# Products of two SBUF tensors offered to GpSimd, and a new table of due dates, in a planned three-stage kernel

## The chip, the cores and the metric

One core of a Trainium2 chip runs the whole program. The metric is the device time of one execution in microseconds (us). Timed executions are given as a median of three; a further execution is recorded by the hardware profiler, and the rows below come from that one.

## What is computed

The reference chains three stages over 4 batches of 768 steps (3072 tokens), 8 heads of 48 columns.

```
for t in range(S):                                   # linear attention with decay w and bonus u
    cur = einsum('bhd,bhe->bhde', u * k_t, v_t)
    y_t = einsum('bhd,bhde->bhe', r_t, state + cur)
    state = w * state + einsum('bhd,bhe->bhde', k_t, v_t)
x = y.transpose(0, 2, 1, 3).reshape(B * S, H * D)
h = x @ w_in                                         # 384 -> 2048
x = softplus(h) @ w_out                              # 2048 -> 384
logits = x @ w_gate                                  # 8 experts, 384 places each
# greedy assignment by falling logit; then, for each expert e,
out[mask] = maximum(x[mask] @ w1[e], 0) @ w2[e]      # 384 -> 1024 -> 384
```

## The kernel before

**Tiling.** The attention is done in 24 steps (called n, 0 to 23), each with 64 time steps of two batches on the 128 partitions. A step loads r, k and v into the tiles rn, kn and vn (two buffers of each, so step n + 2 uses the buffers of step n). It makes ks = kn x pwn[1] and rs = rn x pwn[0], tables of powers of the decay, turns them with TensorE (kT, ar), multiplies them (the masked part goes back into ar), updates the state (wx, copied to X) and multiplies ar with X. The bonus term needs rk = rn x kn, then rk x ut (called rk*ut below), then a sum over columns (sd) that scales vn into sv. Steps 0 to 2 make the bonus on TensorE instead. The sum xf becomes xhl, a pair of float16 halves, and a DMA turns it into xt. Three steps make one block of 384 tokens. Each of the 8 blocks goes through the first feed-forward layer (ffn1, TensorE line 879, 16 slices; ScalarE lines 889 to 891 and VectorE lines 896 and 903 make the softplus) and the second (ffn2, lines 1010 to 1012). The float64 weights of these layers are taken apart on VectorE first (lines 786 to 790). Then the tokens are chosen expert by expert, gathered, multiplied (lines 1504 and 1522 to 1524) and scattered.

**What sets the order.** Nothing is issued as it is written. Every piece of work is recorded as an item with an engine, a planned duration, its dependencies and a due date. `lay_out` then plans all engines once while the program is built: the engine that can start first takes, among the items that could start within SLACK of that moment, the one with the smallest due date plus its entry in the table NUDGE. Items that name several engines in a dictionary go to the one that could start them first, with a handicap: YIELD for VectorE, and BIAS times the difference of planned durations. So each engine's order is fixed when the program is built, and on the chip each engine works through its order and waits on semaphores.

**The shared port in the plan.** The planner keeps a time for VectorE and one for GpSimd in `port`: an item that touches SBUF only on one of them is not planned beside such an item on the other. An item marked `remote` waits for the other's time but doesn't set its own, so that what follows on the other engine may be planned beside it.

```
if eng in port and eng in it.port and not it.remote:
    port[eng] = it.done
```

**Fillers.** Where the plan leaves TensorE without work, `keep_warm` puts matmuls of the tile still into bank 7 (line 184), one for each 56 ns of the planned gap.

**The products.** `product` (line 416) makes ks and rs of steps 1 to 23, and rk and rk*ut of steps 3 to 23: 46 + 42 = 88 products of 128 x 384 float32. Their helper is one line, so the profile has all of them as L416. The zero stores are four items of 96 KB that write zeros to rows of x2d which are read by the first gather.

Of the kernel before, what the change touches and what calls it, by code (L numbers as in the profile page):

```python
# [21 lines left out]
def tile_kernel(ctx, tc, r, k, v, w, u, w_in, w_out, w_gate, w1, w2, out):  # L22
# [18 lines left out]
    PE, ACT, DVE, POOL, SP = nc.tensor, nc.scalar, nc.vector, nc.gpsimd, nc.sync  # L41
# [11 lines left out]


    LAT = 150.0
    SLACK = 87.403
    SAME = {"dve": 130.0, "act": 150.0}
    NBANK = 7
    BIAS = 1.853
    YIELD0 = 218.503  # L60
    YIELD = {"dve": YIELD0}
    WARM = 1e9
    LPH = 6
# [18 lines left out]
    PAIR = (500.0, 1000.0, 2)  # L82
    LANES = 8
    NUDGE = {
# [24 lines left out]
    }  # L109
    LIMIT = {"ph": LPH, "p2": LP2, "att": LATT, "sel": LSEL, "pt": LPT}  # L110
    items, writer, readers = [], {}, {}
# [4 lines left out]
    def banks_of(bank):  # L116
        return [] if bank is None else bank if isinstance(bank, list) else [bank]
# [32 lines left out]
    def op(eng, dur, fn, r=(), w=(), due=0.0, lat=None, bank=None, size=None, small=0):  # L150
        deps = []
        if lat is None:
            lat = LATA[0] if GROUP[0] == "att" else LAT
        for key in r:
            deps.append(writer.get(key))
        for key in w:
            deps.append(writer.get(key))
            deps += readers.get(key, [])
        for b in banks_of(bank):
            deps += b.items  # L160
        it = Item(eng, dur, fn, deps, due, lat, [b for b in banks_of(bank) if not b.items], bank, size)
        for b in banks_of(bank):
            if eng == "pe":
                b.items = [it]
            b.items = b.items[:1] if eng != "pe" else b.items
            b.all.append(it)
        it.small = small
        for key in r:
            readers.setdefault(key, []).append(it)
        for key in w:  # L170
            writer[key] = it
            readers[key] = []
        return it
# [15 lines left out]
    def lay_out(todo, rank, clock, warm=False):  # L189
# [19 lines left out]
        def when(it, eng):  # L209
            at = it.at  # L210
            if eng in port and eng in it.port:
                at = max(at, port["pool" if eng == "dve" else "dve"])
            if len(it.could) > 1:
                at += YIELD.get(eng, 0.0) + BIAS * (it.could[eng] - min(it.could.values()))
            if it.size and eng != "pool":
                k = len(landed) + it.size[2] - 1 - LANES
                if k >= 0:
                    at = max(at, landed[k])
            for b in it.banks:
                for e, t in b.last.items():  # L220
                    if e != eng and eng != "pe":
                        at = max(at, t + LAT)
            if not it.take:
                return at
            k = len(it.take) - 1
            return max(at, sorted(bank_at)[k], sorted(class_at[it.take[0].cls])[k])
# [7 lines left out]
        while any(ready.values()):  # L234
            start, eng = INF, None
            for e, ls in ready.items():
                if ls:
                    t = max(clock[e], min(when(it, e) for it in ls))
                    if t < start:
                        start, eng = t, e  # L240
            it = min((i for i in ready[eng] if when(i, eng) <= start + SLACK),
                     key=lambda i: ((i.small != small) + (not i.small) if eng == "pe" and small else 0, *rank(i)))
# [72 lines left out]
    def begins(blk):  # L315
        return T0 if blk <= 0 else T0 + LEN0 + (blk - 1) * LEN
# [17 lines left out]
    PARTED = 8  # L334
    QUEUES = 1
    UDUE = 2000.0
    ZERODUE = 30000.0
    UTDUE = 6000.0
    HALFL = 12965.117
    HALFL2 = 16904.146  # L340
# [72 lines left out]
    x2d = dram.tile([N, 2 * DM], HF, name="x2d")  # L413

    def product(o, a, b, r, w, due):
        op("dve", 470.0, lambda: DVE.tensor_mul(o, a, b), r=r, w=w, due=due)  # L416


    def scaled(eng, o, a, by):
# [16 lines left out]
    def load_step(n):  # L436
# [52 lines left out]
       w=["gate"], due=T0, size=SMALL)  # L489
# [28 lines left out]
    def factors():  # L518
# [8 lines left out]
       r=["pwt", ("ar", 1, 0)], w=["pwh", ("kT", 1)], due=-1e8)  # L527
    op("dve", 350.0, lambda: DVE.tensor_tensor(PW2[0][..., :C // 2], pwt[:, :, None, :].to_broadcast(twice),
                                               rec[:, :, None, None].to_broadcast(twice), op=OP.mult),
       r=["pwt", ("ar", 1, 0)], w=["pw"], due=-1e8)  # L530
# [22 lines left out]
    def attention(n):  # L553
# [8 lines left out]
        if n:  # L562
            product(ks[:, :, :D], KN[i], PWN[1][:, :, :D], knk + [("pwn", 1), "pads"], [("ks", i)], due)
            product(rs[:, :, :D], RN[i], PWN[0][:, :, :D], rnk + [("pwn", 0), "pads"], [("rs", i)], due + 1)
# [114 lines left out]
        def bonus():  # L679
            product(rk, RN[i], KN[i], rnk + knk, ["rk"], due + 3)  # L680
            product(rk, rk, ut.rearrange("p (h d) -> p h d", h=H), ["ut"], ["rk"], due + 3)
            op("dve", 470.0, lambda: DVE.tensor_reduce(sd, rk, axis=AX.X, op=OP.add), r=["rk"], w=[("sd", i)], due=due + 3)
            op({"dve": 470.0, "act": 1700.0}, 0.0, weighted, r=vnk + [("sd", i)], w=[("sv", i)], due=due + 3)
# [304 lines left out]
    for i in range(2 * NG):  # L988
        b0, s0 = step_tok(NS - NG + i // 2)
        X2S.append(op("sp", 650.0, lambda row=(b0 + i % 2) * S + s0: SP.dma_start(x2d[row:row + 64, :], none),  # L990
                      r=["none"], due=begins(0) + ZERODUE, size=STORE))

# [638 lines left out]
```

## Time and profile before

| | us |
|---|---|
| median of 3 executions (lowest, highest) | 718.51 (718.35, 718.58) |
| the profiled execution | 720.05 |
| its span, first to last instruction | 718.2 |
| around the span | 1.85 |
| mean granted TensorE clock in the span | 0.997 of full speed |

The span is what the rows below divide. The profiled execution took 1.54 us more than the median of the timed ones.

### The profile page before, as it was taken

Reading aid. Unit: us, or ns where it says so; the run is one execution under the profiler, and the core shown is the slowest. Engines: PE = TensorE matmul, PEld = TensorE weight load, DVE = VectorE, ACT = ScalarE, POOL = GpSimd, SP = SyncE. Lnnn points to the kernel's source line nnn. Section 1 sums busy time; section 2 is a strip of 40 time slices with the busy share of each in tenths; the row PEclk is TensorE's granted clock in tenths of the full one; section 3 lists DMA queues with packets and bytes.
Section 4 is the critical chain, followed back from the end, with each engine's and each line's share of the span. In section 5 each row is a group of like instructions: output and inputs, shape, how many; then the busy total and the mean of one; then the engine's idle time right before and its main releaser. Section 6 shows DMA issues by size and latency. Waiting matters only on the chain.

```text
span 718.2 us, 18288 instructions
## 1 busy us (share of the span) xinstructions
PE 707.8 (99%) x7173; PEld 458.5 (64%) x7173; DVE 604.0 (84%) x1638; ACT 401.7 (56%) x889; POOL 63.4 (9%) x107
## 2 busy tenths in 40 slices
PE   9999999999899999999999999999999999999996
PEld 8986666657666666666666566666666665566663
DVE  6999999999898968988899868887799898988630
ACT  4588698674398712689999801311345533524530
POOL 3000000000000000000010000001212422313211
PEclk9999999999999999999999999999999999999998
DMA  6985972445741426512010003442358667647900
GB/s 120 267 202 155 237 149 38 90 86 116 124 77 23 74 52 127 75 29 43 15 23 1 1 13 111 122 143 57 102 143 212 192 155 201 195 124 210 265 34 33
DMA packets 165015, 79.65 MB, mean 111 GB/s; under 512 B 132801, under 2 KB 158273, under 8 KB 164929
## 3 DMA queue, kind: packets, MB, share of 16 engines
q1 hardware_dynamic: 159216, 68.56, 42.0%
q0 software_dynamic: 3072, 9.44, 3.7%
q8 instruction: 56, 0.92, 0.5%
q10 hardware_dynamic: 2640, 0.49, 0.4%
q14 instruction: 31, 0.25, 0.1%
HBM read 60.37 MB, written 9.83 MB: 98 GB/s over the span
## 4 chain that ended last, share of the span: by engine, by line
PE 64%; DVE 15%; issue 12%; DMA 3%; POOL 3%; ACT 2%; POOLq 0%; SPq 0%; DVEq 0%
PE bank L879 20%; PE bank L1010 6%; PE bank L1012 6%; PE bank L1011 6%; PE bank L1504 6%; PE bank L1007 3%; DVE ar L625 2%; PE bank L720 2%; PE bank L184 2%; PE bank L1522 2%; PE bank L1524 2%; PE bank L1523 2%; POOL out L1532 2%; PE bank L615 1%; PE bank L588 1%
## 5 line engine op out<-in xcount | busy, mean ns | idle before, releaser
L879 PEld LDWEIGHTS <-wi 128*128 128x128 f16 x1008 | 98.0, 98 | 65.3 <-issue 1.1
L879 PE MATMUL bank<-xt,wi 128*128 128x384 f16 x672 | 127.6, 326 | 0.1
L1010 PE MATMUL bank<-wo,g 128*128 128x384 f16 (+1 forms) x240 | 78.5, 327 | 0.0
L1012 PE MATMUL bank<-wo,g 128*128 128x384 f16 (+1 forms) x240 | 78.5, 327 | 0.0
L1011 PE MATMUL bank<-wo,g 128*128 128x384 f16 (+1 forms) x240 | 78.4, 327 | 0.0
L879 PE MATMUL bank<-xs,wi 128*128 128x384 f16 x336 | 72.9, 326 | 0.0
L1504 PE MATMUL bank<-g,w1h 128*128 128x384 f16 x384 | 72.8, 325 | 0.0
L889 ACT ACTIVATE ta<-bank 128x384 f32<-128x384 f32 x128 | 61.5, 481 | 17.2 <-PE bank L879 12.9
L896 DVE SCALAR_TENSOR_TENSOR gf<-bank,ta 128x384 f32<-128x384 f32 x112 | 61.6, 551 | 11.2 <-ACT ta L891 10.0
L891 ACT ACTIVATE ta<-ta 128x384 f32<-128x384 f32 x128 | 66.6, 522 | 1.7
L890 ACT ACTIVATE ta<-ta 128x384 f32<-128x384 f32 x128 | 66.4, 522 | 1.5
L1524 PE MATMUL bank<-w2h,g 128*128 128x384 f16 x192 | 62.6, 326 | 0.0
L1523 PE MATMUL bank<-w2l,g 128*128 128x384 f16 x192 | 62.5, 326 | 0.0
L1522 PE MATMUL bank<-w2h,g 128*128 128x384 f16 x192 | 62.5, 326 | 0.0
L1508 ACT ACTIVATE g<-bank 128x384 f16<-128x384 f32 x64 | 31.2, 489 | 43.1 <-PE bank L1504 29.2
L421 ACT ACTIVATE x2o<-bank 128x384 f16<-128x384 f32 x23 | 11.3, 493 | 72.8 <-PE bank L1012 65.3
L1504 PEld LDWEIGHTS <-w1h 128*128 128x128 f16 x384 | 35.5, 97 | 22.9 <-issue 1.0
L903 DVE SCALAR_TENSOR_TENSOR g<-gf,g 128x384 f16<-128x384 f32 x80 | 43.2, 549 | 2.9 <-ACT g L421 2.2
L1511 DVE SCALAR_TENSOR_TENSOR g<-bank,g 128x384 f16<-128x384 f32 x64 | 34.4, 547 | 11.0 <-ACT g L1508 11.0
L1504 PE MATMUL bank<-g,w1l 128*128 128x384 f16 x192 | 41.7, 326 | 0.0
L625 DVE TENSOR_TENSOR ar<-bank,mask 64x256 f32<-64x256 f32 x84 | 35.4, 421 | 4.5 <-PE bank L615 2.7
L1429 POOL DMA_INDIRECT third<-x2d,idx x24 | 25.1, 1044 | 150.7 <-PE bank L1317 124.8
(251 smaller groups left out, 1403.9 us busy)
## 6 DMA issues: line engine op xcount, KB each, us to landing
mraw<-moe_w SPq DMA_DIRECT2D x64, 384.0 KB
third<-moe_w_out SPq DMA_DIRECT2D x8, 768.0 KB
third<-moe_w_in SPq DMA_DIRECT2D x6, 768.0 KB
x2d<-x2o SPq DMA_DIRECT2D x48, 96.0 KB
vn<-v SPq DMA_DIRECT2D x47, 96.0 KB
rn<-r SPq DMA_DIRECT2D x46, 96.0 KB
kn<-k SPq DMA_DIRECT2D x46, 96.0 KB
X<-v SPq DMA_DIRECT2D x36, 96.0 KB
```

Of the source, the lines that this page charges most:

```text
L879: PE.matmul(ph, WF[:, f, a, kk, :], x[:, kk, :], start=(i == 0), stop=(i == 3 * KC - 1))
L889: op("act", 371.0, lambda: ACT.activation(ta, bank.view(BT), AF.Abs), w=[("ta", c)], due=due, bank=bank)
L890: op("act", 413.0, lambda: ACT.activation(ta, ta, AF.Exp, scale=-1.0), w=[("ta", c)], due=due)
L891: op("act", 413.0, lambda: ACT.activation(ta, ta, AF.Ln, bias=1.0), w=[("ta", c)], due=due)
L896: op("dve", 470.0, lambda: DVE.scalar_tensor_tensor(gf, bank.view(BT), 0.0, ta, op0=OP.max, op1=OP.add), r=[("ta", c)], w=[("gf", c)], due ...
L1010: PE.matmul(p, gh[:, f, ts], WU[:, f, 0, :no], start=(f == 0), stop=False)
L1011: PE.matmul(p, gh[:, f, ts], WU[:, f, 1, :no], start=False, stop=False)
L1012: PE.matmul(p, gl[:, f, ts], WU[:, f, 0, :no], start=False, stop=(f == FC - 1))
L1504: PE.matmul(ph, a[:, kk, fs], XH[p][:, x0 + kk, :], start=(i == 0), stop=(i == 3 * KC - 1))
L1522: PE.matmul(po, h1h[:, f, js], w2h[:, fz, :], start=(f == 0), stop=False)
L1523: PE.matmul(po, h1h[:, f, js], w2l[:, fz, :], start=False, stop=False)
L1524: PE.matmul(po, h1l[:, f, js], w2h[:, fz, :], start=False, stop=(f == FB - 1))
```

## The change

A product may now go to GpSimd or VectorE: it names both, at a planned 1150 ns and 490 ns (before 470 ns on VectorE alone), and is marked remote. The due date of the zero stores is moved by 90 us. Three numbers of the planner change a little, and the whole table NUDGE is replaced. Lines behind line 416 of the kernel before stand three lines further down in the changed kernel.

```diff
-    SLACK = 87.403
+    SLACK = 89.403
...
-    BIAS = 1.853
-    YIELD0 = 218.503
+    BIAS = 1.9579999999999997
+    YIELD0 = 207.503
...
     NUDGE = {
-        0: -143448, 1: -197030, 4: -22082, 15: -11678, 16: -12043, 17: -29443, 18: -24752, 19: -1000149502, 20: -1000062522, 21: -10145293,
...
+        1: -363201, 16: -21377, 17: -95815, 18: -86229, 19: -1000139052, 20: -99951731, 21: -10237327, 23: -999934724, 24: -999961413, 43:
...
-    ZERODUE = 30000.0
+    ZERODUE = 120000.0
...
     def product(o, a, b, r, w, due):
-        op("dve", 470.0, lambda: DVE.tensor_mul(o, a, b), r=r, w=w, due=due)
+        op({"dve": 490.0, "pool": 1150.0}, 0.0, lambda eng: (POOL if eng == "pool" else DVE).tensor_mul(o, a, b), r=r, w=w, due=due).remote = True
```

**GpSimd's order, from the factors uw to the first table of the selection.** Before, no product stands here; X_97 is the state that is cleared for step 12.

```order
L519 MEMSET uw 128x8
L521 TENSOR_TENSOR uw<-uq,wt 48x4 x2
L568 MEMSET X_97 64x384
L569 MEMSET X_97 64x384
L1090 IOTA io 128x384
```

In the changed kernel the first products stand behind uw: rs and ks of step 3, rk*ut of step 3, ks and rs of step 5, rk*ut of step 4, ks of step 6, rs and rk of step 9 and rs of step 12.

```order
L522 MEMSET uw 128x8
L524 TENSOR_TENSOR uw<-uq,wt 48x4 x2
L419 TENSOR_TENSOR rs_101<-rn_92,pwn_146 128x8x48
L419 TENSOR_TENSOR ks_103<-kn_94,pwn_147 128x8x48
L419 TENSOR_TENSOR rk_104<-rk_104,ut 128x384
L419 TENSOR_TENSOR ks_103<-kn_94,pwn_147 128x8x48
L419 TENSOR_TENSOR rs_101<-rn_92,pwn_146 128x8x48
L419 TENSOR_TENSOR rk_104<-rk_104,ut 128x384
L419 TENSOR_TENSOR ks_102<-kn_93,pwn_147 128x8x48
L419 TENSOR_TENSOR rs_101<-rn_92,pwn_146 128x8x48
L419 TENSOR_TENSOR rk_104<-rn_92,kn_94 128x384
L419 TENSOR_TENSOR rs_100<-rn_91,pwn_146 128x8x48
```

28 of the 88 products have moved to GpSimd: 11 stand ahead of the clearing of X_97 and 17 behind it; 60 stay on VectorE.

**VectorE's order around ks of step 14.** Before, that product (ks_102) has these rows ahead of it, from rs of step 15 on; wx_113 is the state of step 13 here, and rk_104 the bonus of step 14 (the state of step 12 stands just ahead of these rows).

```order
L416 TENSOR_TENSOR rs_101<-rn_92,pwn_146 128x8x48
L1027 TENSOR_SCALAR LG<-bank_85 128x8
L423 TENSOR_SCALAR xs_120<-xt_118 128x3x128
L423 TENSOR_SCALAR x2o_131<-bank_85 128x384
L416 TENSOR_TENSOR rk_104<-rn_91,kn_93 128x384
L1023 SCALAR_TENSOR_TENSOR x2o_131<-bank_85,x2o_131 128x384
L625 TENSOR_TENSOR ar_112<-bank_86,mask 64x4x64 x2
L653 TENSOR_TENSOR wx_113<-bank_80,wx_113 128x4x48
L416 TENSOR_TENSOR rk_104<-rk_104,ut 128x384
L657 TENSOR_TENSOR wx_113<-wx_113,w_144 128x384
L682 TENSOR_REDUCE sd_105<-rk_104 128x8
L416 TENSOR_TENSOR ks_102<-kn_93,pwn_147 128x8x48
```

In the changed kernel ks of step 14 stands right behind the state of step 12 (bank_82 into wx_113).

```order
L685 TENSOR_REDUCE sd_105<-rk_104 128x8
L419 TENSOR_TENSOR rs_101<-rn_92,pwn_146 128x8x48
L419 TENSOR_TENSOR rk_104<-rn_92,kn_94 128x384
L628 TENSOR_TENSOR ar_112<-bank_83,mask 64x4x64 x2
L654 TENSOR_TENSOR wx_113<-bank_85,w_144 128x4x48
L654 TENSOR_TENSOR wx_113<-bank_82,w_144 128x4x48
L419 TENSOR_TENSOR ks_102<-kn_93,pwn_147 128x8x48
L432 COPY X_98<-wx_113 64x384
L1026 SCALAR_TENSOR_TENSOR x2o_132<-bank_81,x2o_132 128x384
L426 TENSOR_SCALAR xs_120<-xt_118 128x3x128
L1030 TENSOR_SCALAR LG<-bank_81 128x8
L685 TENSOR_REDUCE sd_106<-rk_104 128x8
```

The whole of step 13's state and of step 14's bonus has moved from ahead of ks to behind it or earlier; rk*ut of steps 13 and 15, rs of step 14 and ks of step 15 are now GpSimd's.

## Rows read from the trace of the kernel before

**Rows 1.** The page, sections 1 and 2: engines over the span; tenths in 40 slices

```profile
PE 707.8 (99%) x7173; PEld 458.5 (64%) x7173; DVE 604.0 (84%) x1638; ACT 401.7 (56%) x889; POOL 63.4 (9%) x107
...
DVE  6999999999898968988899868887799898988630
...
DMA  6985972445741426512010003442358667647900
```

**Rows 2.** Busy time by stretch: stretch, length, PE, PEld, DVE, ACT, POOL, clock, DMA, GB/s

```profile
30.00:60.00 30.00, 29.99 (x390) 25.30 (x382) 29.33 (x59) 24.86 (x61) 0.00 (x0) 1.00 0.88 210
60.00:100.00 40.00, 40.00 (x443) 26.78 (x444) 39.27 (x78) 31.24 (x78) 0.00 (x0) 1.00 0.88 194
100.00:150.00 50.00, 49.85 (x495) 30.82 (x493) 49.69 (x115) 41.02 (x104) 0.00 (x0) 1.00 0.38 82
150.00:200.00 50.00, 48.17 (x728) 32.21 (x727) 46.69 (x112) 25.10 (x59) 0.82 (x2) 1.00 0.57 105
200.00:300.00 100.00, 100.00 (x1179) 64.00 (x1178) 85.67 (x198) 60.21 (x144) 0.00 (x0) 1.00 0.42 73
```

**Rows 3.** Waits of PE in the whole span: us in total, times, longest

```profile
PE bank L646 <- DVE ks L416: 1.0, 1, 1.0
PE bank L720 <- DVE ar L625: 0.8, 1, 0.8
```

**Rows 4.** Groups by line: the fillers on PE

```profile
L184 PE MATMUL bank<-still 128*128 128x128 bf16 x204 | 16.1, 235 | 1.0 <-DVE wt L479 1.0
```

**Rows 5.** Timeline of DVE around 187 us: start, us, work

```profile
184.20 0.56 DVE L416 TENSOR_TENSOR rk<-rn,kn 128x384 f32<-128x384 f32 x1 [0.63 <-DMA kn<-k]
...
186.04 0.62 DVE L653 TENSOR_TENSOR wx<-bank,wx 128x192 f32<-128x192 f32 x2
186.58 0.55 DVE L416 TENSOR_TENSOR rk<-rk,ut 128x384 f32<-128x384 f32 x1
...
187.98 1.02 DVE L416 TENSOR_TENSOR ks<-kn,pwn 128x384 f32<-128x384 f32 x2
...
189.49 0.88 DVE L625 TENSOR_TENSOR ar<-bank,mask 64x256 f32<-64x256 f32 x2
```

**Rows 6.** Timeline of PE around 187 us

```profile
187.30 0.33 PE L1012 MATMUL bank<-wo,g 128*128 128x392 f16 x1
188.58 0.68 PE L646 MATMUL bank<-vn,ks 64*64 64x48 f32 x32 [0.95 <-DVE ks L416]
```

**Rows 7.** Groups by line: products, scalings and the second half of g

```profile
L416 DVE TENSOR_TENSOR rs<-rn,pwn 128x384 f32<-128x384 f32 x23 | 12.6, 549 | 1.4 <-DMA rn<-r 1.4
...
L421 ACT ACTIVATE g<-gf 128x384 f16<-128x384 f32 x40 | 20.7, 519 | 2.9 <-DVE gf L896 2.8
...
L423 DVE TENSOR_SCALAR g<-gf 128x384 f16<-128x384 f32 x40 | 14.5, 362 | 0.7
...
L903 DVE SCALAR_TENSOR_TENSOR g<-gf,g 128x384 f16<-128x384 f32 x80 | 43.2, 549 | 2.9 <-ACT g L421 2.2
```

**Rows 8.** Timeline of POOL in the first 7 us

```profile
1.89 0.56 POOL L502 TENSOR_SCALAR identf<-jp 128x128 f32<-128x128 int32 x1
...
5.05 0.41 POOL L574 MEMSET X<- 64x384 f32 x1
...
5.99 0.58 POOL L574 MEMSET X<- 64x384 f32 x1
```

**Rows 9.** Timeline of DVE in the same time

```profile
5.77 0.44 DVE L429 COPY ar<-kT 128x512 f32<-128x512 f32 x1
```

**Rows 10.** Timeline of PE at a change of matmul shape

```profile
230.40 0.33 PE L1011 MATMUL bank<-wo,third 128*128 128x392 f16 x1
230.56 0.33 PE L1012 MATMUL bank<-wo,third 128*128 128x392 f16 x1
230.82 0.68 PE L646 MATMUL bank<-vn,ks 64*64 64x48 f32 x32
```

**Rows 11.** Timeline of SP's queue: the zero stores' first pair

```profile
19.65 2.13 SPq L990 DMA_DIRECT2D x2d<-third  x2
```

49 rows, old and new, of the table NUDGE are left out of this document.

## The prediction

> **What bounds the kernel now.** I read the page first. TensorE's matmuls are busy for 707.8 of 718.2 us, VectorE for 604.0, and GpSimd for 63.4 [rows 1]. But busy matmuls overlap, so 99% doesn't say that nothing is left: the fillers count as busy too. The 204 fillers are busy for 16.1 us, 0.079 us each [rows 4]; 52 of them stand ahead of the first real matmul, while the first loads arrive, which the change leaves as they are. So only the other 152 fillers, about 12 us at 0.079 us each, and the waits of TensorE can be won at all. The rest of the matmuls is the same before and after.
>
> Next I read the stretches, to see where VectorE could be what TensorE waits for. From 30 to 150 us VectorE is busy for 29.33 of 30, 39.27 of 40 and 49.69 of 50 us: it is full. From 150 to 200 us it is busy for 46.69 of 50, and TensorE for 48.17, its largest gap outside the two ends; from 200 to 300 us VectorE has 14 us to spare and TensorE none [rows 2]. Up to 100 us DMA is just as full, 0.88 of its time in both stretches [rows 2]. So relief for VectorE can move the end only if it falls before 200 us, and up to 100 us perhaps not even there.
>
> Then the waits of TensorE by name: two are left that VectorE ends, 1.0 us of L646 for ks and 0.8 us of L720 for ar [rows 3]. Both lie near 187 us: after the last ffn2 matmul at 187.30 us the state matmuls of step 14 start at 188.58 us, 0.95 us of it counted as idle [rows 6]. VectorE has no gap just then. It runs rk, the state, rk*ut and only then ks, at 187.98 us, and reaches the ar that L720 waits for at 189.49 us [rows 5]. This is a queue on VectorE, and products make up much of it.
>
> **What the change does, part by part.**
>
> *Products.* 28 of 88 go to GpSimd. One takes VectorE 549 ns [rows 7], so VectorE loses 28 x 0.549 = 15.4 us. The planner then gives VectorE other work in their place: by the order it makes 8 more scalings (L423), 7 more copies (L429) and 2 more state and bonus scalings, and ScalarE correspondingly fewer. At 0.362 us for a scaling [rows 7], about 0.4 for a copy (the one of 512 columns takes 0.44 [rows 9]) and 0.55 for the others that is 2.9 + 2.8 + 1.1 = 6.8 us. VectorE ends 8.6 us lighter, near 595 us busy. ScalarE loses 8 x 0.519 = 4.2 us for the scalings [rows 7] and some for the rest. ScalarE is not what bounds any stretch [rows 2], so I count that as nothing; the cover is its own idle time, 5 us even in the fullest of these stretches (24.86 of 30).
>
> *Price on GpSimd.* No row shows a product of this shape on GpSimd. From below: a memset of 384 columns, which reads nothing, takes 0.41 us; from above: 128 columns of one input take 0.56 us, and three times that is 1.7 us [rows 8]. I take 1.15 us, the number in the new line, which lies well between; 28 of them fill 32 us of an engine that is idle for 655 us. GpSimd's order has nothing behind the products that is urgent before the gathers, except the clearing of X for step 12 (11 products ahead of it, 17 behind).
>
> *Where it counts.* 11 products leave VectorE before about 165 us, 11 x 0.55 = 6 us, where it is full. I don't credit these: with DMA at 0.88 [rows 2] and, in the new order, 54 fillers still standing among the matmuls of the weight stretch, against 49 before, TensorE is expected to wait for the weights there as it does now. What I credit is the place at 187 us. In the new order ks of step 14 stands right behind the state of step 12. Three products and the state of step 13 that preceded it are elsewhere. I take the whole first wait, 0.95 us [rows 6], and half of the second, 0.4 of 0.8 us [rows 3], since the ar products themselves remain: -1.35 us. Bounds: nothing (a late load takes the place of the queue), and both waits, -1.8 us.
>
> *Changes of matmul shape.* TensorE pays for going from full to small tiles: matmuls of L1011 and L1012 start 0.16 us apart, but the first small one starts 0.26 us after the last of L1012 [rows 10], so 0.1 us a change. The order has 102 such changes before and 92 after: 10 x 0.1 = -1.0 us. Bounds: nothing, where such a change hides a wait that remains, and twice that, -2 us.
>
> *Fillers.* 209 against 204: 5 x 0.079 [rows 4] = +0.4 us at most, nothing if they only fill idle time.
>
> *Zero stores.* By their new due date they would start 90 us later. In SP's order they move only by a few rows: eight DMAs stand between the third and the fourth weight load before (the four stores among them) and eight after (loads of the attention and one store). The first pair takes SP 2.13 us to issue [rows 11], and as much is put in its place, so 0 us. Without that cover it would be one weight load 2 us later or earlier, in the stretch where DMA is full.
>
> *Sum.* -1.35 - 1.0 + 0.4 = -1.95 us. Against the profiled execution, 718.2 us of span and 1.85 around it, 720.05 - 1.95 = 718.1 us. The median of the timed runs stands 1.54 us below the profiled one, so the forecast is 718.5 - 1.95 = **716.6 us**. A change of 0.2%, 1.4 us, is about what a measurement of this kernel can tell from none.
>
> **A rule against it.** What one engine's SBUF access does to the other shows in one place: the memset of X at 5.99 us takes 0.58 us instead of 0.41 [rows 8], while VectorE's copy from SBUF to SBUF runs from 5.77 to 6.21 us [rows 9]. So GpSimd waited for VectorE, for about 0.17 us. The Trainium skill, "SBUF — State Buffer", section "Who interferes with whom", says that a VectorE instruction with two SBUF inputs, or in a two-port mode, and a GpSimd instruction that reads SBUF exclude each other, and that the second to start is blocked until the first has ended. By that rule the products are not free beside VectorE. The trace agrees for a copy that blocks GpSimd; no row shows VectorE held, because GpSimd makes no such product. By the trace's 0.17 us the sum stays; by the rule it is the second rival.
>
> **Rivals.**
>
> *No change that can be told.* The relief up to 200 us is eaten by loads. For it: DMA at 0.88 while VectorE is full [rows 2], and rk at 184.20 us waited 0.63 us for a load of kn [rows 5], so around 187 us loads are late as well. Against it: the fewer shape changes need no relief. Only a part of the 1.0 us and the fillers remain: 718.5 - 0.5 = 718.0 us.
>
> *Slower: VectorE is held by GpSimd's products.* The second half of g, L903, with both inputs in SBUF, runs 80 times at 549 ns [rows 7], and with it the weight preparation, the scalings from SBUF and the remaining products: about every second VectorE instruction could be held. A product of 1.15 us covers two of them, so one is met by most products, and has to wait for something between 0 and 1.15 us, 0.6 to 0.7 on average. For the 11 products in the full stretch that is 7 us more against 6 us saved, and about a third of the 6.8 us taken over from ScalarE, 2.3 us, falls there too: VectorE ends this stretch 3 us late. From 200 us on TensorE has no gap in which to recover [rows 2], so nearly all of it arrives at the end: 718.5 + 3.3 - 1.0 = 720.8 us. The 17 later products cost nothing by themselves, with 14 us of VectorE's time free in 100 [rows 2]. It decides from the point where the mean hold passes the 0.55 us that each product saves.
>
> *The change doesn't do what it says* is excluded: the order shows the 28 products on GpSimd.
>
> **How the numbers follow.** The forecast has 0.43, no change 0.31, held VectorE 0.26. The forecast's own range: both waits gone and 2 us for the shapes, 718.5 - 3.8 = 714.7 us, up to 717.1 us, the bound of what can be told. Holds of the full 1.15 us would add 11 x 0.5 = 5 us to the slower case; half of that is 723, which I leave out together with the far end of the gains. Range 714.5 to 721.6 us. Faster by over 0.2%: 0.43; within: 0.31; slower: 0.26.
>
> **What would show it.** Right: 28 rows of L419 on POOL near 1.15 us each; VectorE's products still near 549 ns, and scalings near 362 ns; VectorE busy near 595 us; no wait of L649 for ks of step 14; the stretch from 150 to 200 us without TensorE's gap of 1.8 us. Wrong: L906 or the products on VectorE with a longer mean or gaps in front of them while POOL runs L419; products on POOL of 1.7 us and more; transposes (L591) waiting for a POOL product; new fillers' stretches followed by waits for weight loads; the clearing of X for step 12 late behind products that wait for a load.

## The result, and the profile after

The changed kernel takes 723.6 us (median of 4 runs, 723.44 to 725.02), the kernel before 718.43 (4 runs) beside it: a ratio of 1.0069, 95% interval 1.0058 to 1.0081. It is slower by about 5 us, where 716.6 was forecast, and it lies outside the range of 714.5 to 721.6. The profiled execution took 723.44 us with a span of 721.6. In the changed kernel the product is L419, the scaling L426, the second half of g L906; in the experiments an edit that adds lines shifts the numbers further (gf, L899 here, is L906 in E2 and L911 in E11 and E12).

First the page of the changed kernel, section 1, which answers to [rows 1].

```profile
PE 710.1 (98%) x7178; PEld 460.7 (64%) x7178; DVE 605.0 (84%) x1627; ACT 397.3 (55%) x862; POOL 92.4 (13%) x135
```

GpSimd is 29 us busier and ScalarE 4.4 us lighter, about as expected. But VectorE, which gave away 28 products, is busy for 605.0 us, 1 us more than before. The forecast had 595. That is the first line to stop at.

The same kernel by stretch; the columns are those of [rows 2].

```profile
30.00:60.00 30.00, 28.86 (x424) 25.05 (x422) 29.22 (x56) 26.57 (x67) 3.96 (x4) 1.00 0.84 205
60.00:100.00 40.00, 39.78 (x455) 26.04 (x454) 39.54 (x76) 30.98 (x85) 0.00 (x0) 1.00 0.93 213
100.00:150.00 50.00, 49.30 (x451) 30.87 (x449) 49.43 (x111) 41.05 (x97) 2.28 (x2) 1.00 0.36 74
150.00:200.00 50.00, 49.21 (x530) 31.07 (x529) 41.85 (x95) 26.71 (x61) 6.06 (x7) 1.00 0.34 63
200.00:300.00 100.00, 98.95 (x1354) 64.73 (x1353) 85.61 (x200) 54.96 (x127) 11.40 (x11) 1.00 0.50 93
```

TensorE's gap from 150 to 200 us shrinks from 1.83 to 0.79 us, as predicted, but the stretch no longer holds the same work: the state matmuls of steps 12 to 14, at 177 to 189 us before, stand at 202 to 214 us now. New gaps stand at 30 to 60 (1.14 us), 100 to 150 (0.70) and 200 to 300 us (1.05), where there was next to nothing [rows 2].

The waits of TensorE name who ends them (us in total, times, longest):

```profile
PE bank L649 <- DVE gf L899: 0.7, 1, 0.7
PE bank L753 <- DVE xf L740: 0.6, 1, 0.6
PE bank L882 <- DVE x2o L1026: 0.5, 1, 0.5
PE bank L618 <- DVE gf L899: 0.5, 1, 0.5
PE bank L882 <- DVE wx L656: 0.5, 2, 0.3
PE bank L875 <- DVE wi L793: 0.5, 1, 0.5
```

The two waits of [rows 3] are gone. These six have come, all ended by VectorE, 3.3 us in sum.

What does VectorE do beside a product on GpSimd? The timeline of GpSimd in the changed kernel:

```profile
27.01 1.04 POOL L419 TENSOR_TENSOR rk<-rk,ut 128x384 f32<-128x384 f32 x1 [5.35 <-DMA ut<-u]
...
127.85 1.32 POOL L419 TENSOR_TENSOR rk<-rn,kn 128x384 f32<-128x384 f32 x1
...
198.79 1.00 POOL L419 TENSOR_TENSOR rs<-rn,pwn 128x384 f32<-128x384 f32 x1 [29.57 <-PE bank L591]
...
206.69 1.00 POOL L419 TENSOR_TENSOR ks<-kn,pwn 128x384 f32<-128x384 f32 x1 [2.67 <-PE bank L649]
```

and of VectorE at the same times:

```profile
26.16 0.55 DVE L791 SCALAR_TENSOR_TENSOR wi<-third,wi 128x384 int32<-128x384 int32 x1
26.63 0.55 DVE L660 TENSOR_TENSOR wx<-wx,w 128x384 f32<-128x384 f32 x1
27.10 1.37 DVE L793 SCALAR_TENSOR_TENSOR wi<-third,wi 128x384 int32<-128x384 int32 x1
...
127.60 0.71 DVE L419 TENSOR_TENSOR ks<-kn,pwn 128x384 f32<-128x384 f32 x1
128.24 1.35 DVE L677 TENSOR_TENSOR sv<-vn,sd 128x384 f32<-128x384 f32 x1
...
199.05 0.96 DVE L426 TENSOR_SCALAR xhl<-xf 128x384 f16<-128x384 f32 x1
...
206.35 0.54 DVE L685 TENSOR_REDUCE sd<-rk 128x8 f32<-128x384 f32 x1
206.91 1.31 DVE L628 TENSOR_TENSOR ar<-bank,mask 64x256 f32<-64x256 f32 x3
```

Read the two together. GpSimd starts at 27.01 us and ends at 28.05; L793 starts at 27.10 on VectorE and ends at 28.47, 0.42 us after GpSimd. Its own work of 0.55 us has been pushed back until GpSimd was done. The same holds for L677 (1.35 instead of 0.55) and for a scaling with one input, L426 (0.96 instead of 0.36 [rows 7]). All ten two-input instructions of 384 or 392 columns that were pushed back end 0.41 to 0.43 us after the product that held them. At 206.69 us nothing is pushed: a reduction was running, then three L628, which read a bank of PSUM, 1.31 us for three in a row. GpSimd suffers as well: 1.32 us at 127.85, where VectorE's ks was running first.

Over the 28 products, 13 instructions on VectorE are longer by more than 0.1 us than their kind is undisturbed, 6.9 us in sum (0.16 to 0.83 each). 15 products hold nothing; beside them stand reductions, work on banks, and instructions that were running first.

### The profile page after: what moved, and what is told of

The parts are those of the page before. It is cut to its first block, busy times and chain, and to the rows that moved or that the text cites. A ratio compares the mean times of both kernels' runs of the same rounds, so it can differ in the third digit from the quotient of the medians.

```text
span 721.6 us, 18319 instructions
## 1 busy us (share of the span) xinstructions
PE 710.1 (98%) x7178; PEld 460.7 (64%) x7178; DVE 605.0 (84%) x1627; ACT 397.3 (55%) x862; POOL 92.4 (13%) x135
## 4 chain that ended last, share of the span: by engine, by line
PE 72%; issue 11%; DVE 8%; ACT 4%; POOL 3%; SPq 1%; DMA 0%; POOLq 0%; DVEq 0%
PE bank L882 20%; PE bank L1013 7%; PE bank L1015 7%; PE bank L1014 7%; PE bank L1507 7%; PE bank L1010 4%; PE bank L723 2%; PE bank L1525 2%; PE bank L1526 2%; PE bank L1527 2%; PE bank L187 2%; POOL out L1535 2%; PE bank L591 1%; PE bank L649 1%; PE bank L618 1%
## 5 line engine op out<-in xcount | busy, mean ns | idle before, releaser
L899 DVE SCALAR_TENSOR_TENSOR gf<-bank,ta 128x384 f32<-128x384 f32 x112 | 61.5, 552 | 11.9 <-ACT ta L894 10.8
L906 DVE SCALAR_TENSOR_TENSOR g<-gf,g 128x384 f16<-128x384 f32 x80 | 43.4, 551 | 2.4 <-ACT g L424 1.7
L1466 DVE SCALAR_TENSOR_TENSOR w2l<-mraw,w2h 128x768 f16<-128x768 f32 x32 | 30.4, 953 | 9.2 <-ACT w2h L1462 9.2
```

Source lines behind the costliest of these rows:

```text
L899: op("dve", 470.0, lambda: DVE.scalar_tensor_tensor(gf, bank.view(BT), 0.0, ta, op0=OP.max, op1=OP.add), r=[("ta", c)], w=[("gf", c)], due ...
```

## The experiments

Each ratio is to runs of the kernel before on the same chip, whose medians there are 719.33 us (E1, E2, E4, E5), 719.19 (E6, E7, E8, E10) and 719.14 (E11, E12, E13).

### E1: the new order, all products on VectorE

```diff
-        op({"dve": 490.0, "pool": 1150.0}, 0.0, lambda eng: (POOL if eng == "pool" else DVE).tensor_mul(o, a, b), r=r, w=w, due=due).remote = True
+        op({"dve": 490.0, "pool": 1150.0}, 0.0, lambda eng: DVE.tensor_mul(o, a, b), r=r, w=w, due=due).remote = True
```

> The changed kernel with its order kept, but the 28 products that the plan gives to GpSimd are issued on VectorE at the same places. No GpSimd product is left, so VectorE is held nowhere, and it gets 28 x 0.55 = 15.4 us of work back. Theory A (the loss is VectorE held by GpSimd's products, 6.9 us in all in the trace of the changed kernel): the holds go, the work comes back, and where both fall in the full stretches it is a net loss of some 4 us: 724 to 728 us. Theory B (the new order itself loses the time, at 27 to 85 us and 195 to 230 us, with or without holds): also 724 to 728 us, or more. The run measures what the offer to GpSimd is worth in this order: at 723.6 us or less it is worth nothing.

Measured: 725.09 us, ratio 1.0088 (1.0072 to 1.0105). Its page:

```profile
PE 709.8 (98%) x7178; PEld 459.8 (64%) x7178; DVE 611.1 (85%) x1655; ACT 396.9 (55%) x862; POOL 62.9 (9%) x107
```

The order takes VectorE 611.1 - 604.0 = 7.1 us more when it makes everything itself; that is the work taken over from ScalarE, priced at 6.8 in the prediction. GpSimd's products, with their holds, bring the ratio down by only 0.0019, some 1.4 us, and the two intervals overlap. E1 has no holds and is the slower of the two: in this order VectorE's own work costs as well, 6.3 us at the end beside the kernel before.

### E2: the new order, memsets on GpSimd in place of its products

```diff
+        def made(eng):
+            if eng == "dve":
+                DVE.tensor_mul(o, a, b)
+            else:
+                POOL.memset(o, 0.0)
+                POOL.memset(o, 0.0)
```

> The changed kernel with its order kept; the 28 products on GpSimd are left out and two memsets of the same tile stand in their place, which write as much and take about as long (some 0.9 us) but read nothing. Theory A (VectorE is held because GpSimd reads two SBUF tensors): VectorE's stretched instructions fall back to their usual 0.55 us, and most of the 6.9 us of holds that fall before 230 us comes back: 718 to 720 us. Theory B (the order itself): 722.5 to 723.6 us. If VectorE is held by any GpSimd instruction on SBUF, reads or not: no change, with the holds still to be seen.

Measured: 719.28 us, ratio 1.0004 (0.9987 to 1.0021). Its page, section 1:

```profile
PE 707.6 (99%) x7178; PEld 459.1 (64%) x7178; DVE 598.8 (83%) x1627; ACT 397.2 (55%) x862; POOL 86.3 (12%) x163
```

One of its groups of memsets on GpSimd, by line:

```profile
L424 POOL MEMSET ks<- 128x384 f32 x10 | 4.2, 419 | 0.6
```

And its timeline of VectorE, beside a pair of memsets that GpSimd starts at 126.28 and 126.75 us:

```profile
126.14 0.55 DVE L421 TENSOR_TENSOR ks<-kn,pwn 128x384 f32<-128x384 f32 x1
126.61 0.55 DVE L684 TENSOR_TENSOR sv<-vn,sd 128x384 f32<-128x384 f32 x1
127.07 1.01 DVE L906 SCALAR_TENSOR_TENSOR gf<-bank,ta 128x384 f32<-128x384 f32 x2
```

A pair of memsets with its gap ends 0.89 us after its start, so what waits for the tile waits about as long as for a product. But the same sv that took 1.35 us takes 0.55, and VectorE is 6.2 us less busy than in the changed kernel, close to the 6.9 us of holds. The time falls back to that of the kernel before. So it is the products' exclusion with VectorE that costs, 1.0069 - 1.0004 or some 4.7 us. E2 takes away GpSimd's own delays too, but no wait in the list of the changed kernel's trace is put down to GpSimd.

Both kernels run the same 7178 matmuls in the same order, so the starts in the two profiled executions can be compared one by one. The changed kernel falls behind E2 by 0.76 us at one wait for VectorE and by 0.92 at another:

```profile
30.91 0.55 PE L753 MATMUL bank<-identf,xf 128*128 128x128 f32 x3 [0.59 <-DVE xf L740]
132.71 0.68 PE L649 MATMUL bank<-vn,ks 64*64 64x48 f32 x30 [0.70 <-DVE gf L899]
```

At 133 us it is 2.4 us behind, at 320 us 4.1, and at the last matmul 3.9. From 320 us on the distance no longer grows, so the later stages, which work on other values in E2 because products are left out, add nothing to it.

E2 also says something that no theory had: even with the products gone from both engines the new order is no faster than the old (1.0004, interval around 1). Its windows show where the predicted gain went:

```profile
30.00:60.00 30.00, 29.79 (x424) 25.63 (x422) 28.78 (x57) 27.24 (x69) 3.22 (x8) 1.00 0.94 226
60.00:100.00 40.00, 39.77 (x461) 26.22 (x459) 39.45 (x76) 30.13 (x83) 0.84 (x2) 1.00 0.83 202
100.00:150.00 50.00, 50.00 (x456) 30.98 (x455) 49.50 (x113) 42.72 (x100) 0.84 (x2) 1.00 0.38 79
150.00:200.00 50.00, 49.95 (x594) 31.88 (x595) 41.59 (x100) 25.89 (x58) 5.83 (x14) 1.00 0.35 65
200.00:300.00 100.00, 98.75 (x1357) 64.68 (x1356) 83.72 (x198) 55.00 (x125) 9.51 (x23) 1.00 0.51 91
```

And so does the longest of its waits of TensorE:

```profile
PE bank L625 <- DVE gf L906: 1.3, 1, 1.3
```

The gap of 1.83 us before 200 us [rows 2] is closed to 0.05, and one of 1.25 us opens after it.

### E11 and E12: the early and the late products apart

```diff
+            MADE[0] += 1
+            if MADE[0] > 11:            # E12: <= 11
+                POOL.tensor_mul(o, a, b)
+            else:
+                POOL.memset(o, 0.0)
+                POOL.memset(o, 0.0)
```

> The changed kernel with the first 11 of GpSimd's 28 products (up to about 155 us) left out, two memsets of their tile in their place; the 17 later ones are made as in the changed kernel. Their holds up to 155 us add up to 3.8 us, those of the 17 later ones to 3.1 us (five instructions on VectorE, at 167 to 275 us). If the holds of the full stretch alone arrive at the end and the later ones are free, as the prediction had it: the time of the kernel without any of the 28, 719.3 us, within 0.5. If a hold costs wherever VectorE has a queue, also after 155 us: between that and the changed kernel's 723.6, near 721.0.

> The other half: the first 11 products are made on GpSimd as in the changed kernel, the 17 from 167 us on are left out, two memsets in place of each. If only the early holds arrive at the end: 723.6 us, as the changed kernel, within 0.5. If early and late ones both do: near 721.5 us. If it is the late holds alone, beside TensorE's waits for VectorE at 195 to 230 us: near 719.5.

Measured: with the late 17 alone (E11) 720.52 us, ratio 1.0024 (1.0015 to 1.0034); with the early 11 alone (E12) 722.55 us, 1.0052 (1.0039 to 1.0065). Above E2 that is 1.4 us for the late and 3.5 us for the early ones, 4.9 us together beside the 4.7 of all 28. The early ones count clear of noise. E11's interval overlaps E2's, so the times alone don't settle the late ones; the traces point the same way. Matmul by matmul the profiled execution of E11 is 0.9 us behind E2's where the late products begin (lost before 66 us, where the two kernels are alike, so by chance) and 2.7 us behind at 272 us. So the late ones are probably not free, though VectorE has 14 us to spare there. One place shows how. VectorE in E11:

```profile
222.30 1.38 DVE L918 SCALAR_TENSOR_TENSOR third<-gf,third 128x384 f16<-128x384 f32 x1
223.61 0.55 DVE L911 SCALAR_TENSOR_TENSOR gf<-bank,ta 128x384 f32<-128x384 f32 x1
```

and TensorE in E11, with its wait in brackets:

```profile
224.21 0.69 PE L630 MATMUL bank<-ar,kT 64*64 64x64 f32 x30 [2.01 <-DVE gf L911]
```

and in E2, at the same matmul:

```profile
222.19 0.69 PE L625 MATMUL bank<-ar,kT 64*64 64x64 f32 x30 [1.25 <-DVE gf L906]
```

A product that starts on GpSimd at 222.27 us holds L918 for 0.83 us; gf, which frees the bank that TensorE waits for, comes right behind it, and TensorE's wait grows from 1.25 to 2.01 us. (In the changed kernel the same matmul waits only 0.51 us, at 225.75: there L906 had ended just before the product began, and another instruction was held.) The average slack of a stretch doesn't protect the one instruction that is urgent.

### E13: only the 15 products that held nothing

```diff
+            MADE[0] += 1
+            if MADE[0] in (1, 4, 11, 12, 15, 16, 17, 20, 21, 23, 24, 25, 26, 27, 28):
+                POOL.tensor_mul(o, a, b)
+            else:
+                DVE.tensor_mul(o, a, b)
```

> The changed kernel's order with only those 15 products on GpSimd that held nothing on VectorE; the 13 that did are made on VectorE in the same places. A product on VectorE takes 0.55 us of it and the 13 holds were 0.53 us each on average, so by busy time alone VectorE stands as in the changed kernel. If holds and products cost alike: 723.5 us, within 0.7. If a hold costs more than a product, because it falls on whichever instruction is urgent: 721 to 722. If what GpSimd took off VectorE is worth more than the holds cost: 724 to 725, towards the kernel with all products on VectorE (725.1).

Measured: 723.02 us, ratio 1.0054 (1.0041 to 1.0067), not to be told from the changed kernel. Its page has VectorE where the changed kernel has it:

```profile
PE 710.1 (99%) x7178; PEld 460.5 (64%) x7178; DVE 604.9 (84%) x1640; ACT 397.4 (55%) x862; POOL 79.1 (11%) x122
```

13 products more on VectorE and 13 holds fewer cancel: a product that holds VectorE brings nothing. (Two of the 15 now meet something, 0.8 us in sum.) Against E1, all on VectorE, the 15 are worth 1.0088 - 1.0054, some 2.4 us.

### E5 and E8: the old order

Here the plan of before is kept, and products by their number in the order go to GpSimd: in E5 the same 28 as in the changed kernel, in E8 12 of them beside which VectorE, with all 28 on GpSimd, showed nothing stretched.

```diff
+        MADE[0] += 1
+        eng = POOL if MADE[0] in ON_POOL else DVE
+        op("dve", 470.0, lambda: eng.tensor_mul(o, a, b), r=r, w=w, due=due)
```

> The kernel before with its plan kept, except that the same 28 products are issued on GpSimd, each at its old place in the program. VectorE loses 15.4 us of work and is held for some 7 us. Theory A in its simple form (holds decide): slower than before, 720 to 723 us. Theory B (the new order carries the loss, the moved products are a net relief): 716 to 718.5 us.

> The kernel before with its plan kept, and on GpSimd only those 12 products beside which, in the run with 28, VectorE showed nothing stretched (it did work from PSUM there). Theory A (it is the holds that cost, and a product that holds nothing relieves VectorE by 0.55 us): no stretched instruction, VectorE 6.6 us lighter, and the time at that of before or up to 1.5 us below: 717 to 718.5 us on a chip where before takes 718.4. If any product on GpSimd costs by its own length (0.45 us longer for who waits): slower than before.

Measured: E5 721.9 us, ratio 1.0045 (1.0029 to 1.006); E8 718.91 us, ratio 0.9992 (0.9979 to 1.0004). E5 pays without any new order. VectorE in E5, while GpSimd makes two products in a row (from 39.66 and from 40.63 us, the second 1.31 us long):

```profile
39.72 1.36 DVE L662 TENSOR_TENSOR wx<-wx,w 128x384 f32<-128x384 f32 x1
41.01 1.75 DVE L793 SCALAR_TENSOR_TENSOR wi<-third,wi 128x768 int32<-128x768 int32 x1
```

The engines take turns: wx waits for the first product, the second product for wx, and wi for the second product. E8 has no instruction on VectorE beside a product that is more than 0.1 us longer than its kind's median. Its page:

```profile
PE 707.6 (99%) x7173; PEld 459.2 (64%) x7173; DVE 599.3 (84%) x1626; ACT 402.5 (56%) x889; POOL 76.5 (11%) x119
```

VectorE is 4.7 us lighter than before, and the time is at best 0.2% less: the old order has almost no use for that time where it came free.

### E10: copies in place of the products

As E2, with two copies of one operand on GpSimd instead of two memsets:

```diff
+                POOL.tensor_copy(o, a)
+                POOL.tensor_copy(o, a)
```

> The changed kernel with its order kept; the 28 products on GpSimd are left out and two copies of the first factor stand in their place, each with one SBUF input. It tells whether VectorE is held by any GpSimd instruction that reads SBUF, or by two inputs alone. Theory A as the trace suggests it (the second to start waits, for as long as the first runs): VectorE's instructions with two SBUF inputs are stretched beside each copy, 720 to 723.6 us by the length of the copies. If only two inputs hold: as with memsets, near the time of before.

Measured: 720.5 us, ratio 1.0015 (1.0002 to 1.0028), which overlaps E2's interval. The trace tells more than the time. VectorE beside a copy that starts on GpSimd at 127.07 us and takes 0.77 us (0.51 where nothing meets it):

```profile
127.39 0.86 DVE L684 TENSOR_TENSOR sv<-vn,sd 128x384 f32<-128x384 f32 x1
```

Reading one tensor on GpSimd is enough to hold VectorE; a shorter instruction holds for less.

### E4, E6 and E7: one part alone, replanned

E4 is the kernel before with the product's line alone:

```diff
-        op("dve", 470.0, lambda: DVE.tensor_mul(o, a, b), r=r, w=w, due=due)
+        op({"dve": 490.0, "pool": 1150.0}, 0.0, lambda eng: (POOL if eng == "pool" else DVE).tensor_mul(o, a, b), r=r, w=w, due=due).remote = True
```

E6 is the kernel before with the zero stores' date alone:

```diff
-    ZERODUE = 30000.0
+    ZERODUE = 120000.0
```

E7 is the changed kernel without `remote`:

```diff
-        op({"dve": 490.0, "pool": 1150.0}, 0.0, lambda eng: (POOL if eng == "pool" else DVE).tensor_mul(o, a, b), r=r, w=w, due=due).remote = True
+        op({"dve": 490.0, "pool": 1150.0}, 0.0, lambda eng: (POOL if eng == "pool" else DVE).tensor_mul(o, a, b), r=r, w=w, due=due)
```

> The kernel before with the new line of product alone; the old due dates, the old table and the old place of the zero stores stay, and the planner lays out anew and sends some 20 products to GpSimd. Theory A: each is held or holds as in the changed kernel, 0.25 us of VectorE each, and the order is not fitted to it: 719 to 723 us. Theory B (the new table carries the loss): 717 to 719 us.

> The kernel before with the new due date of the zero stores alone; the planner moves the four stores and with them a few loads. Theory: they lie beside other DMAs of the same length, so the time is that of before within 0.7 us. A rival: the loads that take their place come in another order, and the first weight pieces reach VectorE later or earlier: 2 us either way.

> The changed kernel without the mark remote on the products, so that the planner keeps what touches SBUF on VectorE away from a product on GpSimd, as it does for other GpSimd work; the due dates stay, though they were fitted to the other plan. Theory A: the stretched instructions all but vanish. How many products still go to GpSimd and where the order puts them decides the time: 720 to 726 us, the shortfall of a table that doesn't fit included.

Measured: E4 726.53 us, ratio 1.0106 (1.0089 to 1.0123); E6 723.9, 1.0051 (1.0032 to 1.007); E7 731.08, 1.0158 (1.013 to 1.0185). All three lie above the times expected, and in E7 the stretched instructions have not vanished: beside its 33 products 11 instructions of VectorE are more than 0.1 us longer than their kind's median, 5.9 us in sum, though the plan keeps the two engines apart. These three don't test the part that they name. Each makes the planner work out another plan, for which the table of due times was not made; the fillers of E4 show it:

```profile
L184 PE MATMUL bank<-still 128*128 128x128 bf16 x255 | 20.1, 239 | 1.0 <-DVE wt L479 1.0
```

They are 255 in E4, 256 in E6 and 339 in E7, against 204 [rows 4] in the kernel before and 209 in the changed one. That the plans alone cost the time is argued, not shown. So what the later zero stores cost or bring by themselves stays open.

## Why the prediction was wrong, point by point

**The step that failed** is the one that set the products' cost beside VectorE at nothing: "By the trace's 0.17 us the sum stays". The only row for it, one memset delayed behind a copy [rows 8, 9], showed GpSimd held by VectorE, and its 0.17 us were small because VectorE's copy had only 0.22 us left when the memset began. What is held waits for the end of the whole instruction in front of it, so the size is set by GpSimd's 1.0 us. The rule that was weighed against the row was right: the Trainium skill, "SBUF — State Buffer", section "Who interferes with whom", has VectorE's instructions with two SBUF inputs and GpSimd's instructions that read SBUF exclude each other, and VectorE's two-port modes exclude GpSimd. The traces agree, with holds of 0.16 to 0.83 us beside products, and with none of a two-input instruction beside memsets (E2) or of work on banks or reductions beside products (E8). Of the miss of 7.0 us (723.6 against 716.6) this step is 4.7 us (E2); nearly all of the rest is the 1.95 us of gains, which E2, with no product that could hold, does not show.

**The rival that came true** is the second, but its price of 720.8 us was 2.8 us short, and its terms were not what the trace has. The mean hold is 0.25 us over the 28 products (6.9 / 28), as only 13 of them hold anything, and near 0.34 over the early 11, not 0.6 to 0.7. Its point of decision, 0.55 us, was not reached, yet the kernel is slower. Two reasons. A product saves less than its duration: products start 0.47 us apart where VectorE runs full (126.14 and 126.61 in E2), and 28 of them are worth 611.1 - 598.8 = 12.3 us of busy time, 0.44 each, not 0.549. And the work of the new order costs far more than the 2.3 us that the rival gave to what VectorE takes over: with every product on VectorE it stands 6.3 us above the kernel before (E1). Taking the 28 products off VectorE brings 6.0 us of that back (E1 to E2), and the exclusion costs 4.7 (E2 to the changed kernel): 6.3 - 6.0 + 4.7 = 5.0 us, the loss measured. How much of the 6.3 us is the work from ScalarE and how much the order no run separates. The rival's 17 free later products come to 1.4 us (E11), not clear of noise. The range ended at 721.6, below the 723 us that the prediction worked out for longer holds and left out.

**VectorE's busy time** then adds up: 604.0, plus 7.1 taken over (E1), less 12.3 for the products, is 598.8 (E2); 6.2 more with the holds is 605.0. The forecast's 595.4 had the products too dear by 3.1 us, and no holds.

**The place at 187 us** was read rightly, as a place: the waits of [rows 3] are gone, also at 214.4 us, where the state matmuls of step 14 now stand. The smaller gap from 150 to 200 us says less, since steps 12 to 14 have left that stretch. It was wrong to book 1.35 us at the end. One step on, behind the state matmuls of step 15, TensorE waits 1.25 us for VectorE's gf in E2, and for gf again in the changed kernel (L618, 0.5 us at 225.75), where it had no wait before. So what E2 wins at step 14 it loses for the most part at step 15. That this is the old queue on VectorE, moved on, is likely but not shown.

**Changes of matmul shape and fillers.** The -1.0 us and the +0.4 us were not tried apart. The price of a change holds in the changed kernel (the first small matmul again starts 0.26 us after the last full one, in the median), but [rows 10] shows it only from full to small, and the 102 and 92 changes count both directions, 51 and 46 of each. With all other terms, they come to 1.0004 in E2, where the sum without holds says 0.9973. 0.9973 lies outside E2's interval, so at least part of that sum didn't arrive; how much of it is the shapes' is open.

**What was right:** the products' price on GpSimd (1.00 us undisturbed, means of 1.03 to 1.16 by operand, 1.15 taken); ScalarE's relief bringing nothing that the waits show (no run tests it alone); DMA no obstacle to be seen in the waits; the list of signs, of which "the products on VectorE with a longer mean" and the longer second halves of g showed.

**Against the first rival**, no change that can be told: its cause, late loads, is not what the waits show. But its time, 718.0 us, is near what the kernel would take if GpSimd's products held nothing (1.0004 in E2, 718.7 us).

## What to carry to other kernels

An engine that is idle for 90% of the time is not a free one: ask what its instruction shares with the engine that it is to relieve, and if they exclude each other, count the holding as up to the whole length of the foreign instruction, on whatever instruction is next, urgent or not. Here work moved to GpSimd brought something only where VectorE read PSUM or reduced meanwhile (15 products of 28, worth 2.4 us against the same order with all on VectorE; the other 13 nothing), and in the old order twelve such products brought nothing that can be told (E8). An order that is planned for such an offer has a price of its own: here 6.3 us, which ate the 6.0 us that the products gave back. And a stall closed in one place is a gain only if none opens in another: follow the steps behind it before booking it.

## What the runs showed of the hardware that I had not expected

- VectorE's scalings with a single SBUF input are held too, not only products: to f16, 0.96 us instead of 0.36 (L426 at 199.05 us).
- GpSimd's copies, with one input, hold VectorE as well (0.86 instead of 0.55 us in E10). Its memsets hold no two-input instruction of VectorE (E2), but they and VectorE's one-input scalings delay each other: in E2 a scaling that meets a memset takes 0.47 us instead of 0.35 (25.04 us), and memsets that meet a scaling take 0.51 and 0.57 us instead of 0.42 (25.35 and 222.66 us).
- GpSimd is itself delayed: 1.00 us becomes 1.32 at 127.85 us, and in E12 one product takes 2.03 us.
- A VectorE product of 0.55 us costs the engine only 0.47 us in a row of its like, since each starts before the one ahead has ended (126.14 and 126.61 us in E2).
